# Issuing one buffer's regrouping transfers a step earlier in a spectral-mixing and SoLU kernel

## The chip, the core and the metric

The kernel runs on one core of a Trainium2 chip. A core has five engines with instruction streams of their own: TensorE (PE) multiplies matrices into PSUM, VectorE (DVE) and ScalarE (ACT) do elementwise work, GpSimd (POOL) does elementwise work on SBUF, and SyncE (SP) issues DMA transfers. ACT and POOL can issue transfers too. Each engine works through its instructions in the order in which the program gives them, and waits on semaphores for the other engines and for transfers.

The metric is the time in microseconds of one execution, the median of several.

## The reference

Two blocks follow each other. The first filters along the sequence in the frequency domain, the second is a two-layer network whose activation is `h * softmax(h)` with a layer norm.

```python
# first block: x (8, 3136, 256), filters (1569, 256)
X = np.fft.rfft(x, axis=1)
y = np.fft.irfft(X * (filt_r + 1j * filt_i)[None], n=3136, axis=1)
# second block: x = y as (25088, 256), w_in (256, 1024), w_out (1024, 256)
h = x @ w_in
sm = softmax(h)                      # over the 1024
solu = h * sm
ln = (solu - mean(solu)) / np.sqrt(var(solu) + 1e-6) * g_ln
out = ln @ w_out
```

All of it is float32.

## The kernel before

**Stages.** The Fourier transform is split into matrix products with tables over 49 and 64 points. The sequence of batch element 0 is transformed first. Then one main loop runs, and in it the transforms of elements 1 to 7 are woven between the steps of the network for the tokens that are ready. The table `PLAN` says in which step each piece of a transform stands.

**The network.** The 25,088 tokens are 196 tiles of 128. Two tiles are a *pair* (98 pairs), and two pairs are a *group* (49 groups). For a pair, each of the two layers is computed with seven block products in place of eight (Strassen's scheme in Winograd's form), so sums of blocks are formed by POOL: `pair_sums` for the first layer, `project_sums` for the second.

**Steps.** The main loop calls `step(k)`, with `j, odd = divmod(k, 2)`: two steps, an even and an odd one, for a pair j. One step takes about 7 us. The order of instructions on every engine is the order in which `step` writes them (`tc.manual_schedule()`); no scheduler moves them. A pair goes through these places:

- The first-layer products (line 723) of pair j stand in steps 2j and 2j+1. ACT and DVE bring the results from PSUM to SBUF (`keep`, line 733, and `finish`, lines 744 and 747).
- `exponential` (line 755), `normalize` (line 771), `square` (line 779) and `turn` (line 787) follow for each tile, some steps later. `turn` transposes 32 x 32 blocks on DVE and writes the tile's part of the group's buffer `turn`. The last `turn` of a group with pairs 2g and 2g+1 stands in step 4g+6.
- `regroup(p, i)` (line 799) finishes the transposition with four transfers from `turn` to `solu_t`, from SBUF to SBUF, 128 KB each. There are two destination buffers for a pair, i = 0 and i = 1 (tags `solu_t0`, `solu_t1`), each double-buffered, so that pair p writes where pair p-2 has been. SP issues all of them. Both calls for pair p stand in the even step 2(p+3).
- `deviations` (lines 806 to 810) computes the reciprocal deviations of a group and writes them to DRAM (`rows`) in step 4g+6. `regroup_deviations` (line 816) reads them back with four small transfers, `rs_t`, in the odd step 4g+7. For the last group POOL issues these, otherwise SP.
- `project_sums` (line 702) forms the sums on POOL in step 2(p+4). The first sum reads the second buffer of `solu_t`, and the next the first buffer.
- The second-layer products (line 844) 1, 2, 6 and 7 of pair p stand in the odd step 2(p+4)+1, and products 5, 3 and 4 in the even step after it. Product 1 and 2 read the first buffer of `solu_t`, 4 the second. ACT (`keep_out`, line 856) and DVE (`finish_out`, line 860) scale the results with `rs_t`; the first use of a group's `rs_t` is ACT's instruction after product 1 of the group's first pair. Product 6 adds to the PSUM bank that this ACT instruction reads, so it comes after it.
- `store_out` (line 868) writes the pair's output with two transfers at the end of an even step.

**Other transfers.** SP also issues loads of `x` for the later elements (line 245, four at a time, placed after the stores). ACT issues the loads of `t` (512 KB, line 291) and of the table `de` (line 683), POOL the rest. Transfers of SP and ACT use eight completion semaphores in turn; a transfer that is to use one waits first until the transfer before it on the same semaphore has landed.

**Around the change.** In an odd step the part of `step` that the change touches stands after products 3 and 4 and ahead of `regroup_deviations`; in an even step, after the second-layer product 4 and the loads of `t` and `de`.

Of the kernel before, what the change touches and what calls it, by code (L numbers as in the profile page):

```python
# [94 lines left out]
def kernel(  # L95
# [88 lines left out]
    class Spectrum:  # L184
# [114 lines left out]
        def product(self, i, out, lhsT, rhs):  # L299
            for v in range(self.units[i][1]):  # L300
                nc.tensor.matmul(out=out[:, v, :], lhsT=lhsT(v), rhs=rhs[:, v, :],  # L301
                                 start=True, stop=True)
# [401 lines left out]
    def pair_sums(j):  # L704

        s14 = upool.tile([P, 2, P], FP32, name=f"s14_{j}", tag="s14")
        s23 = wk.tile([P, 2, P], FP32, name=f"s23_{j}", tag="s23")
        sums[j] = s1, s2, s3, s4 = s14[:, 0, :], s23[:, 0, :], s23[:, 1, :], s14[:, 1, :]
        a11, a12, a21, a22 = (tokens(2 * j + i, c) for i in range(2) for c in range(KD))
        sum_of(s1, a21, a22, ALU.add)  # L710
        sum_of(s2, s1, a11, ALU.subtract)
        sum_of(s3, a11, a21, ALU.subtract)
        sum_of(s4, a12, s2, ALU.subtract)
# [15 lines left out]
    def keep(j, k, i):  # L729

        if k not in hs:
            hs[k] = hpool.tile([P, DFF], FP32, name=f"h_{k}", tag=f"h{k % 2}")
        nc.scalar.copy(out=h_half(k, i), in_=ms[j, 0])  # L733

    def finish(j, k, i, kept, bank):


        if k not in nmaxs:
            nmaxs[k] = small.tile([P, 2], FP32, name=f"nmax_{k}", tag=f"nmax{k % 2}")
            sofar, to = 3.0e38, nmaxs[k][:, 0:1]  # L740
        else:
            sofar, to = nmaxs[k][:, 0:1], nmaxs[k][:, 1:2]
        if kept is None:
            nc.vector.tensor_scalar(out=h_half(k, i), in0=ms[j, bank], scalar1=0.0, scalar2=sofar,
                                    op0=ALU.add, op1=ALU.min, accum_out=to)
        else:
            nc.vector.tensor_tensor_reduce(out=h_half(k, i), in0=ms[j, bank], in1=h_half(*kept),  # L747
                                           scale=1.0, scalar=sofar, op0=ALU.add, op1=ALU.min,
                                           accum_out=to)
# [40 lines left out]
    def regroup(p, i):  # L790


        g, second = divmod(p, 2)
        turned = turns[g].rearrange("p (k q) b i -> p k q (b i)", q=4)
        a = 2 * second + i
        st = upool.tile([P, KF, P], FP32, name=f"solu_t_{p}_{i}", tag=f"solu_t{i}")
        solu_ts[p, i] = st[:, 0:KF // 2, :], st[:, KF // 2:KF, :]
        for q in range(4):
            nc.sync.dma_start(out=st[32 * q:32 * q + 32, :, :],  # L799
                              in_=turned[32 * a:32 * a + 32, :, q, :])  # L800
# [17 lines left out]
    def project_sums(p, step):  # L818

        (a11, a12), (a21, a22) = solu_ts[p, 0], solu_ts[p, 1]  # L820
        if step == 0:
            s1 = upool.tile([P, KF // 2, P], FP32, name=f"u1_{p}", tag="u1")
            sum_of(s1, a21, a22, ALU.add)
            sum_of(a21, a11, a21, ALU.subtract)
            solu_sums[p] = s1, None, a21, None
        else:
            s2 = spool.tile([P, KF // 2, P], FP32, name=f"u2_{p}", tag="u2")
            s4 = spool.tile([P, KF // 2, P], FP32, name=f"u4_{p}", tag="u4")
            s1, _, s3, _ = solu_sums[p]
            sum_of(s2, s1, a11, ALU.subtract)  # L830
            sum_of(s4, a12, s2, ALU.subtract)
            solu_sums[p] = s1, s2, s3, s4
# [21 lines left out]
    def keep_out(p, i, to):  # L854
        rs = out_half(p, i, 0)[1]
        nc.scalar.activation(out=out_half(p, *to)[0], in_=pos[p, 0], func=AFT.Copy, scale=rs)  # L856
# [89 lines left out]
    pairs = blocks // 2  # L946

    def step(k):
        j, odd = divmod(k, 2)
        p = j - (LAG - 1) // 2 if odd else j - (LAG + 1) // 2  # L950
        if not 0 <= p < pairs:
            p = None
        hid, proj = k < blocks, p is not None
        if not odd and 2 <= j - 4 < pairs:
            project_sums(j - 4, 0)
        if k < LAG:
            if not odd:
                product(j, 1)
                keep(j, k, 0)
                product(j, 2)  # L960
                finish(j, k, 0, (k, 0), 1)
            else:
                product(j, 5)
                keep(j, k - 1, 1)
                finish(j, k, 1, (k - 1, 1), 2)
        for job in top[k] + stores[k] + products[k]:
            job()
        if not odd and 0 <= j - 4 < 2:
            project_sums(j - 4, 0)
        if odd and j + 1 < pairs:  # L970
            pair_sums(j + 1)
        if not odd:
            if hid and k > LAG:
                product(j, 1)
                keep(j, k, 0)
            if 2 <= k < blocks:
                exponential(k - 2)
            if proj:
                project(p, 5)
                keep_out(p, 1, (0, 1))  # L980
            if blocks <= k < blocks + 2:
                exponential(k - 2)
            if hid and k > LAG:
                product(j, 2)
            if 3 <= k < blocks + 3:
                turn(k - 3)
            if hid and k > LAG:
                finish(j, k, 0, (k, 0), 1)
            if proj:
                finish_out(p, 1, 1, (0, 1), 1)  # L990
            for job in early[k]:
                job()
            if 3 <= k < blocks + 3:
                square(k - 3)
            if hid:
                product(j, 6)
                keep(j, k + 1, 0)
            if proj:
                project(p, 3)
                keep_out(p, 0, (0, 1))  # L1000
                project(p, 4)
            for job in spectrum_loads[k]:
                job()
            if 0 <= j - 3 < pairs:
                regroup(j - 3, 0)
                regroup(j - 3, 1)
            if j - 3 == pairs - 2:
                deviations(j - 3, nc.gpsimd.dma_start)
            if 0 <= j - 4 < pairs:
                project_sums(j - 4, 1)  # L1010
            if j - 3 == pairs - 2:
                regroup_deviations((j - 3) // 2, nc.gpsimd.dma_start)
            elif 0 <= j - 3 < pairs:
                deviations(j - 3, nc.sync.dma_start)
            if hid:
                product(j, 7)
            if 2 <= k < blocks + 2:
                normalize(k - 2)
            for job in second_parts[k] + middle[k] + first_parts[k]:
                job()  # L1020
            if proj:
                finish_out(p, 1, 0, (1, 0), 1)
                store_out(p)
        else:
            if hid and k >= LAG:
                product(j, 5)
                keep(j, k - 1, 1)
                finish(j, k, 1, (k - 1, 1), 2)
            for job in early[k]:
                job()  # L1030
            if proj:
                project(p, 1)
                keep_out(p, 0, (0, 0))
                project(p, 2)
                finish_out(p, 0, 0, (0, 0), 1)
            if 2 <= k < blocks + 2:
                exponential(k - 2)
            if hid:
                product(j, 3)
                product(j, 4)  # L1040
            if 0 <= j - 3 < pairs:
                if (j - 3) % 2 == 0 and j - 3 < pairs - 2:
                    regroup_deviations((j - 3) // 2, nc.sync.dma_start)
            if proj:
                project(p, 6)
                project(p, 7)
            for job in second_parts[k] + middle[k]:
                job()
            if 3 <= k < blocks + 3:
                turn(k - 3)  # L1050
            if hid:
                finish(j, k - 1, 1, None, 0)
                finish(j, k, 0, (k, 0), 2)
            if 2 <= k < blocks + 2:
                normalize(k - 2)
            if proj:
                keep_out(p, 1, (1, 0))
            if 3 <= k < blocks + 3:
                square(k - 3)
            for job in first_parts[k]:  # L1060
                job()
        for job in late[k] + loads[k]:
            job()
        if k < 2:
            for n in ((0, 1), range(2, 7))[k]:
                prepare_w_out(n)
# [37 lines left out]
```

## Time and profile before

The kernel took 1629.31 us, the median of three runs (1626.2 to 1629.95). The profiled execution took 1631.3 us, of which the span from the first to the last instruction is 1629.5.

| engine | busy us | share of the span |
|---|---|---|
| PE | 1551.8 | 95% |
| DVE | 1306.9 | 80% |
| POOL | 1167.1 | 72% |
| ACT | 903.7 | 55% |

| transfers | issued by | how many | KB each |
|---|---|---|---|
| `solu_t` <- `turn`, line 799 | SP | 784 | 128 |
| `out_dram` <- `ot`, line 868 | SP | 196 | 128 |
| `x` <- input, line 245 | SP | 208 | 98 or 128, 16 of 30 |
| `rs_t` <- `rows`, line 816 | SP | 192 | 0.5 |
| `rs_t` <- `rows`, line 816 | POOL | 4 | 0.5 |
| `rows` <- `rs`, line 810 | SP | 48 | 2 |

Busy time is the time in which an engine works on an instruction; issuing a transfer isn't counted. In the lists of waits each line names the waiting engine and line, what it waited for, and the total in microseconds, how often, and the longest. "SPq" is SP's queue of issues. In a timeline a line gives start, length, engine, line, operation and tile of one or more like instructions, and in brackets the idle time before it with what ended it. For a transfer the length is that of its issue by the engine, not that of the data's way.

### The profile page before, as it was taken

Reading aid. Unit: us, or ns where it says so; the run is one execution under the profiler, and the core shown is the slowest. Engines: PE = TensorE matmul, PEld = TensorE weight load, DVE = VectorE, ACT = ScalarE, POOL = GpSimd, SP = SyncE. Lnnn points to the kernel's source line nnn. Section 1 sums busy time; section 2 is a strip of 40 time slices with the busy share of each in tenths; the row PEclk is TensorE's granted clock in tenths of the full one; section 3 lists DMA queues with packets and bytes.
Section 4 is the critical chain, followed back from the end, with each engine's and each line's share of the span. In section 5 each row is a group of like instructions: output and inputs, shape, how many; then the busy total and the mean of one; then the engine's idle time right before and its main releaser. Section 6 shows DMA issues by size and latency. Waiting matters only on the chain.

```text
span 1629.5 us, 37007 instructions
## 1 busy us (share of the span) xinstructions
PE 1551.8 (95%) x12710; PEld 1048.1 (64%) x12710; DVE 1306.9 (80%) x2630; ACT 903.7 (55%) x1772; POOL 1167.1 (72%) x1333
## 2 busy tenths in 40 slices
PE   4898889999999999999999999999999999999997
PEld 1362456666666677667766676666776777777776
DVE  1686778998899889897989888988888777777772
ACT  2235555566565665566656655566556666566662
POOL 4446786688777877697678866788667776677775
PEclk8899999999999999999999999999999999999999
DMA  9887878776888778866787668766875454444443
GB/s 264 251 277 241 237 213 224 216 217 190 208 232 228 205 184 246 225 189 172 207 238 213 187 168 222 230 182 164 224 210 168 128 130 129 104 108 105 112 107 105
DMA packets 377245, 312.13 MB, mean 192 GB/s; under 512 B 62762, under 2 KB 342835, under 8 KB 377059
## 3 DMA queue, kind: packets, MB, share of 16 engines
q1 hardware_dynamic: 304340, 168.63, 40.1%
q0 software_dynamic: 34624, 101.68, 20.9%
q10 hardware_dynamic: 38096, 39.46, 8.2%
q8 instruction: 103, 1.69, 0.4%
q14 instruction: 82, 0.67, 0.1%
HBM read 124.86 MB, written 81.50 MB: 127 GB/s over the span
## 4 chain that ended last, share of the span: by engine, by line
PE 61%; DMA 8%; POOL 3%; DVE 2%; issue 2%; SPq 2%; ACT 1%; ACTq 0%; POOLq 0%; DVEq 0%
PE o L844 28%; PE m L723 27%; DMA solu_t<-turn 4%; PE py L372 3%; PE pa L269 2%; DMA x<-in_x_dram 1%; PE pb L301 1%; PE pc L301 1%; POOL u L702 1%; SPq L799 1%; DMA t<-d 1%; DMA out_dram<-ot 1%; DMA rs_t<-rows 1%; POOL x L260 1%; DVE turn L787 0%
## 5 line engine op out<-in xcount | busy, mean ns | idle before, releaser
L844 PEld LDWEIGHTS o<-w_out_sb,solu_t 128*128 128x128 f32 x3136 | 382.7, 192 | 51.5 <-issue 43.1
L844 PE MATMUL o<-w_out_sb,solu_t 128*128 128x128 f32 x3136 | 402.4, 276 | 4.9 <-DVE ot L860 2.1
L723 PE MATMUL m<-w_in_sb,s 128*128 128x512 f32 x784 | 396.3, 606 | 7.8 <-ACT h L733 7.5
L844 PEld LDWEIGHTS o<-w_out_sb,u 128*128 128x128 f32 x2352 | 308.6, 192 | 144.4 <-issue 105.9
L723 PE MATMUL m<-w_in_sb,y 128*128 128x512 f32 x588 | 309.6, 610 | 11.7 <-DVE nmax L747 9.2
L844 PE MATMUL o<-w_out_sb,u 128*128 128x128 f32 x2352 | 312.9, 276 | 6.2 <-ACT ot L856 3.6
L733 ACT COPY h<-m 128x512 f32<-128x512 f32 x294 | 173.2, 589 | 241.0 <-PE m L723 194.6
L771 DVE SCALAR_TENSOR_TENSOR h<-e,rsum,h 128x1024 f32<-128x1024 f32 x196 | 301.3, 1537 | 6.9
L702 POOL TENSOR_TENSOR u<-solu_t 128x512 f32<-128x512 f32 x98 | 132.9, 1356 | 236.2 <-DMA solu_t<-turn 139.9
L856 ACT ACTIVATE ot<-o,rs_t 128x128 f32<-128x128 f32 x392 | 143.9, 367 | 262.8 <-PE o L844 244.6
L779 ACT ACTIVATE h<-h,nmu 128x1024 f32<-128x1024 f32 x196 | 225.0, 1148 | 58.2 <-DVE turn L787 47.9
L747 DVE CUSTOM_DVE_ANT_0 h<-m,h 128x512 f32<-128x512 f32 x196 | 133.9, 683 | 145.3 <-ACT h L733 104.5
L787 DVE STREAM_TRANSPOSE turn<-h 128x1024 f32<-128x1024 f32 x196 | 243.1, 1240 | 3.2
L755 ACT ACTIVATE e<-h,nmax 128x1024 f32<-128x1024 f32 x196 | 225.2, 1149 | 9.1 <-DVE h L771 8.7
L702 POOL TENSOR_TENSOR u<-solu_t,u 128x512 f32<-128x512 f32 x98 | 150.7, 1538 | 88.4 <-PE o L844 84.1
L723 PEld LDWEIGHTS m<-w_in_sb,s 128*128 128x128 f32 x784 | 128.2, 191 | 95.1 <-issue 85.4
L723 PEld LDWEIGHTS m<-w_in_sb,y 128*128 128x128 f32 x588 | 96.7, 192 | 111.4 <-issue 52.6
L702 POOL TENSOR_TENSOR u<-u,solu_t 128x512 f32<-128x512 f32 x98 | 159.5, 1627 | 0.9
L860 DVE SCALAR_TENSOR_TENSOR ot<-o,rs_t,ot 128x128 f32<-128x128 f32 x294 | 101.8, 346 | 71.7 <-ACT ot L856 51.3
L702 POOL TENSOR_TENSOR solu_t<-solu_t,solu_t 128x512 f32<-128x512 f32 x98 | 152.7, 1558 | 7.7
L702 POOL TENSOR_TENSOR s<-y 128x128 f32<-128x128 f32 x196 | 95.8, 489 | 0.4
L372 PEld LDWEIGHTS py<-wb_t,t 50*64 50x64 f32 x3584 | 57.6, 134 | 42.9 <-issue 21.7
(116 smaller groups left out, 1970.6 us busy)
## 6 DMA issues: line engine op xcount, KB each, us to landing
solu_t<-turn SPq DMA_DIRECT2D x784, 128.0 KB
out_dram<-ot SPq DMA_DIRECT2D x196, 128.0 KB
t<-d POOLq DMA_DIRECT2D x112, 200.0 KB, 6.1
d<-x POOLq DMA_DIRECT2D x100, 200.0 KB, 5.3
f<-f_dram POOLq DMA_DIRECT2D x39, 512.0 KB, 7.0
d<-g POOLq DMA_DIRECT2D x39, 512.0 KB, 4.7
t<-d ACTq DMA_DIRECT2D x37, 512.0 KB
x<-in_x_dram SPq DMA_DIRECT2D x112, 98.0 KB
```

The lines of the kernel that those rows point to most:

```text
L372: nc.tensor.matmul(out=views[g][64 * h:64 * h + 64, cb, i, :], lhsT=t4[rows, i, c0:c0 + 64], rhs=wb_t[rows, 0:N1], start=True, stop=True)
L702: nc.gpsimd.tensor_tensor(out=out, in0=in0, in1=in1, op=op)
L723: nc.tensor.matmul(out=ms[j, bank], lhsT=lhsT, rhs=w_in_sb[:, w, :], start=m in (1, 2, 7), stop=True, skip_group_check=True)
L733: nc.scalar.copy(out=h_half(k, i), in_=ms[j, 0])
L747: nc.vector.tensor_tensor_reduce(out=h_half(k, i), in0=ms[j, bank], in1=h_half(*kept), scale=1.0, scalar=sofar, op0=ALU.add, op1=ALU.min, ...
L755: nc.scalar.activation(out=e, in_=hs[k], func=AFT.Exp, bias=nmaxs.pop(k)[:, 1:2], scale=-1.0, accum_out=esum)
L771: nc.vector.scalar_tensor_tensor(out=solu, in0=e, scalar=rsum, in1=solu, op0=ALU.mult, op1=ALU.mult, accum_out=nmu)
L779: nc.scalar.activation(out=solu, in_=solu, func=AFT.Square, bias=nmu, scale=-float(DFF), accum_out=variances[g][:, i:i + 1])
L787: nc.vector.transpose(out=turns[g][:, :, i, :], in_=solus[k].rearrange("p (f j) -> p f j", j=32))
L844: nc.tensor.matmul(out=pos[p, bank], lhsT=lhs[:, f, :], rhs=w[:, f, :], start=f == 0 and m in (1, 2, 7), stop=True, skip_group_check=True)
L856: nc.scalar.activation(out=out_half(p, *to)[0], in_=pos[p, 0], func=AFT.Copy, scale=rs)
L860: nc.vector.scalar_tensor_tensor(out=ot, in0=pos[p, bank], scalar=rs, in1=out_half(p, *kept)[0], op0=ALU.mult, op1=ALU.add)
```

## The change

For the second pair of each group (odd p), `regroup(p, 0)` moves from the even step 2(p+3) to the odd step before it, 2(p+2)+1, ahead of `regroup_deviations`. `regroup(p, 1)` stays in the even step. For the first pair of a group both calls stay. What is transferred is the same.

```diff
@@ step, even part
             for job in spectrum_loads[k]:
                 job()
             if 0 <= j - 3 < pairs:
-                regroup(j - 3, 0)
-                regroup(j - 3, 1)
+                for i in range((j - 3) % 2, 2):
+                    regroup(j - 3, i)
             if j - 3 == pairs - 2:
                 deviations(j - 3, nc.gpsimd.dma_start)
@@ step, odd part
             if hid:
                 product(j, 3)
                 product(j, 4)
+            if j % 2 and 0 <= j - 2 < pairs:
+                regroup(j - 2, 0)
             if 0 <= j - 3 < pairs:
                 if (j - 3) % 2 == 0 and j - 3 < pairs - 2:
                     regroup_deviations((j - 3) // 2, nc.sync.dma_start)
```

## The prediction

> **What bounds the kernel now.** I write R0 for the four transfers of line 799 into the first buffer (`solu_t`, i = 0) of a group's second pair, R1 for the four into its second buffer, "rs loads" for the four small loads of line 816, and p for the pair number (0 to 97; second pairs are odd). Page first: which engine is full.
>
> ```profile
> span 1629.5 us, 37007 instructions
> ...
> PE 1551.8 (95%) x12710; PEld 1048.1 (64%) x12710; DVE 1306.9 (80%) x2630; ACT 903.7 (55%) x1772; POOL 1167.1 (72%) x1333
> ```
>
> Then the busy time by stage, columns: stretch, length, PE, PEld, DVE, ACT, POOL (each with its count), granted clock, DMA share, GB/s.
>
> ```profile
> 300.00:500.00 200.00, 194.81 (x1743) 132.29 (x1735) 176.37 (x337) 116.15 (x230) 148.79 (x171) 1.00 0.79 215
> ...
> 900.00:1100.00 200.00, 194.24 (x1674) 133.54 (x1674) 170.26 (x336) 116.54 (x230) 147.90 (x172) 0.98 0.72 197
> ...
> 1200.00:1400.00 200.00, 200.00 (x1760) 143.40 (x1753) 160.41 (x348) 119.26 (x235) 139.17 (x159) 1.00 0.54 144
> ```
>
> PE is the bound. From about 1130 us (the last `x` load is issued at 1107.0) its first gap above 0.25 us is at 1587.7, in the drain; a transfer there is worth nothing unless it is late. From 300 to 1100 us it idles 16.2 us in all (800 less 194.81, 196.87, 197.90 and 194.24), and from 165 to 300 another 14.2. So a gain has about 30 us to draw on. Who waits for the transfers concerned (total us, times, longest):
>
> ```profile
> POOL u L702 <- DMA solu_t<-turn: 139.9, 39, 9.9
> ...
> ACT ot L856 <- DMA rs_t<-rows: 14.3, 7, 5.3
> ...
> PEld m L723 <- DVE nmax L747: 23.3, 28, 3.4
> ```
>
> The waits of the SP queue itself, and its order around two second pairs, p = 43 (with `x` loads) and p = 75 (without):
>
> ```profile
> SPq L799 <- DMA t<-d: 42.2, 13, 7.0
> ...
> SPq L816 <- DMA rows<-rs: 29.3, 16, 3.9
> ```
>
> ```profile
> 858.53 1.32 SPq L868 DMA_DIRECT2D out_dram<-ot  x2
> 859.96 2.54 SPq L245 DMA_DIRECT2D x<-in_x_dram  x4
> 863.72 1.74 SPq L816 DMA_DIRECT2D rs_t<-rows  x4
> 865.80 8.29 SPq L799 DMA_DIRECT2D solu_t<-turn  x8
> ```
>
> ```profile
> 1333.35 2.12 SPq L816 DMA_DIRECT2D rs_t<-rows  x4
> 1335.56 7.68 SPq L799 DMA_DIRECT2D solu_t<-turn  x8
> 1343.34 0.61 SPq L868 DMA_DIRECT2D out_dram<-ot  x1
> ```
>
> The reader is to see that R0 and R1 follow the rs loads without a gap: SP is behind, and R0 waits for its place, not for data.
>
> [...] an `rs_t` issue takes 0.42 us (median), its landing comes 4.3 us after it. [...]
>
> **The change part by part.** Nothing is added or removed; 4 × 49 transfers move. PE, ACT, DVE and POOL keep their instruction order. The source is ready: the group's last transpose (line 787) stands one step earlier. The buffer's last reader is product 2 of pair p−2, earlier in the same odd step (for p = 75 it ends at 1330.6), and the wait on it is the same as before. So on SP the order after the stores and `x` loads turns from rs, R0, R1 into R0, rs, R1. For the last pair (p = 97), whose rs loads are issued by POOL, SP's order is unchanged, so the drain's last chain is too.
>
> *R0 earlier*: by the four rs issues, about 1.8 us, plus the wait for `rows`. Who needs R0? POOL's second sum of the pair, which stands behind its first sum, and that reads R1. In every second pair POOL's first sum starts 0.1 to 0.9 us after R1's landing (1345.6 and 1345.7 for p = 75). Worth nothing by itself.
>
> *R1*: still behind both R0 and rs. In the tail it waits for product 4 of pair p−2 (1340.6 for p = 75, R1 issued at 1340.7), so it doesn't move. In the loading stage it starts 0.1 to 8 us after that product (2.0 for p = 33) and could move up by the part of the `rows` wait that R0 now fills. Where a `t` load of 512 KB stands between, SP waits for it (42.2 us in all) before R0's third transfer or so, with five or six issues of 0.65 us behind it; afterwards only two are behind. R1 then lands about 2 us earlier. But PE's gaps that POOL ends come to 4.1 us after 200 us (four, 0.33 to 2.06). Gain: 0 to 4 us; I take 1.5.
>
> *rs later*: by R0's issue, 4 × 0.65 = 2.6 us, and by a second thing. SP and ACT transfers use eight completion semaphores in turn, and a transfer waits until the one before it on its semaphore has landed. In the built program the rs loads follow R1 of the first pair there in 100 of 192 cases before; after, they follow `x` loads in 71, the stores in 53, R0 itself in 20. So where four `x` loads stand ahead, the last rs load is issued only after the last of them landed. The trace's semaphore updates give each landing (the last update on a transfer's semaphore before the next transfer is issued on it), so this can be done pair by pair: last `x` landing + 4.3 us (median landing of `rs_t` before 1130 us, 120 loads, quartiles 3.7 and 5.3), against ACT's first use (line 856). p = 43: 867.2 + 4.3 = 871.5 against 868.3, 3.2 late. p = 33: 711.4 + 4.3 = 715.7 against 714.1, 1.6 late. p = 21: 2.9 late; p = 13: 2.3. Over the 20 second pairs with `x` loads ahead (p = 3 to 59) the lateness is 0.2 to 3.2, in sum about 27 us. In before the same loads land 0.1 to 3.2 us ahead of use; the longest of the seven that came late is
>
> ```profile
> 1059.88 0.37 ACT L856 ACTIVATE ot<-o,rs_t 128x128 f32<-128x128 f32 x1 [5.35 <-DMA rs_t<-rows]
> ```
>
> *What hides it, and what is late next.* Behind the waiting ACT instruction stand the exponential and later evictions, and DVE's line 860. PE's product 6 needs that ACT read, and starts 2.04 us after its end in most groups. DVE's next eviction of a first-layer bank (line 744) ends 0.1 to 2.2 us before PE needs the bank (median about 1.1), with 0.5 us idle before line 860. So 1.1 to 2.0 us are hidden. Taking off each group's own cover (the smaller of 2.0 and 0.5 plus its DVE slack), PE loses 1.8 (p = 21), 2.1 (p = 43), 0.9 (p = 55), 0.8 (p = 29), 0.6 (p = 31, like 55 without cover, since it is late already), 0.4, 0.3 and 0.2: 7.1 us. Without any cover it would be 27. If landing takes 1 us more[...], most groups pass their cover: about 18 us; 2 us more, about 36.
>
> *Tail, p over 60*: no `x` loads. For p = 75: R0 from 1332.4, rs 1335.0 to 1336.9, landed by about 1341.5, used at 1343.3. The slack of 1.9 to 6.8 us before falls by 2.6; only p = 95 (1.9) and the start (p = 1, 0.1) go below nothing. With the drain and the start uncovered: 0.5 and 1.5 us.
>
> **Sum.** +7.1 +2.0 −1.5 = +7.6 us. Against the profiled execution: span 1629.5 to 1637.1, its own time 1631.3 to 1638.9; it lies 2.0 above the median of 1629.3, so the median becomes **1637 us**.
>
> **The rivals.** (1) *R1 sooner, PE fed better: faster.* For it: POOL's 139.9 us of waiting, and 42.2 us of SP waits on `t`. If POOL 2 us earlier also lets its `x` and first-layer sums go sooner, half of the 16.2 us of PE idle goes: 1621 us. It decides if ACT's wait for rs stays under its cover everywhere; against it: PE waited only 4.1 us for POOL, and SP's queue is no shorter. (2) *All of it hidden: no change.* PE absorbed p = 31 in before (ACT 1.5 us late, no PE gap above 0.25 us within 10 us). If rs lands in 3.7 us instead of 4.3, the loss is about 3 + 2.0, less the gain: 1631. (3) *A heavy loss.* Landing of rs behind R0 2 us longer: +36, 1666; with 1 us, 1648. (4) That the order on SP doesn't change is excluded by the built program.
>
> **How the numbers follow.** Small loss as summed, with up to 1 us of longer landing (1634.5 to 1648): 0.45. Heavy loss: 0.13. No change: 0.22. Faster: 0.20. A difference of 0.3% (4.9 us) is about what a measurement can tell from none. The range 1621 to 1654 leaves out the far half of the heavy losses and gains beyond half of the idle time; the likeliest case's own range is 1634 to 1648.
>
> **What would show it.** Right: rs loads behind R0 in the SP timeline; ACT line 856's wait on `rs_t` from 14.3 to 30 us or more, nearly all before 1130 us; PE idle from 300 to 1100 us above 16.2; the tail's PE packed as before; SP's wait on `rows` at line 816 mostly gone. Wrong: ACT's `rs_t` wait about the same, or PE idle smaller with POOL's wait on `solu_t` well under 140 us.

## The result

The changed kernel took 1650.11 us, the median of five runs (1643.86 to 1657.83), against 1629.31 for the kernel before (five runs, 1621.96 to 1632.52): 1.0131 times as long, with a 95% interval of 1.0105 to 1.0156, or 20.8 us more. A loss was forecast and the time lies in the range, but the loss is nearly three times the 7.6 us of the sum. The profiled execution is the slowest of the five: 1657.8 us with a span of 1656.1, 26.6 more than before's span.

First the page's span and busy times, and the busy time by stage (columns as in the prediction).

```profile
span 1656.1 us, 36845 instructions
...
PE 1560.0 (94%) x12710; PEld 1057.3 (64%) x12710; DVE 1287.9 (78%) x2630; ACT 904.3 (55%) x1772; POOL 1159.4 (70%) x1333
```

```profile
300.00:500.00 200.00, 192.74 (x1817) 131.37 (x1810) 170.38 (x336) 115.19 (x228) 145.13 (x173) 0.98 0.78 210
500.00:700.00 200.00, 189.64 (x1732) 130.96 (x1734) 161.84 (x331) 110.84 (x222) 140.80 (x168) 0.97 0.75 209
...
900.00:1100.00 200.00, 194.94 (x1685) 133.11 (x1678) 164.19 (x339) 117.38 (x234) 145.33 (x171) 0.98 0.72 198
...
1200.00:1400.00 200.00, 200.00 (x1798) 143.22 (x1797) 165.42 (x357) 119.12 (x235) 137.98 (x163) 1.00 0.58 158
```

The tail is packed as it was; the loss lies in the stage with `x` loads. The offset between the two executions, taken at the first `keep_out` of a group, grows from +7.1 us at p = 1 to +27.9 at p = 59 and is +25.9 at p = 95.

The 26.6 us can be split without a remainder. PE is busy 1560.0 against 1551.8, so 8.2 us longer for the same 12,710 matmuls, and idle 96.1 against 77.7 (span less busy), so 18.4 us more. Of the idle time 4.0 us fall before 165 us (38.65 against 34.69), where no transfer has moved yet; they belong to this execution and not to the change. 2.0 fall from 165 to 300, 10.9 from 300 to 1100 and 1.5 after it. Without the first 4.0 us, 22.6 are left to explain, close to the 20.8 of the medians.

Now who waits, in the list of waits of the changed kernel.

```profile
POOL u L702 <- DMA solu_t<-turn: 139.0, 49, 8.8
...
ACT ot L856 <- DMA rs_t<-rows: 46.8, 15, 7.6
...
PE o L844 <- ACT ot L856: 28.9, 17, 5.3
...
PEld m L723 <- DVE nmax L747: 7.4, 16, 1.5
```

ACT's wait for `rs_t` went from 14.3 to 46.8 us (another 19.9 are put down to `solu_t`; in this trace 42 of SP's 192 rs loads come next after a `solu_t` transfer on their completion semaphore), and PE's product 6 now waits 28.9 us for that ACT instruction (3.6 before). The wait that shrank is PE's for DVE's `nmax`, from 23.3 to 7.4. The traces of both kernels show what a shared semaphore does: SP and ACT go through eight, and in each trace 1,614 issues come next after another transfer on one, and none begins before that transfer's last update there (0.016 us after it at the least).

The groups of PE's instructions from 300 to 1100 us show both at once: matmuls that read POOL's sums `u` in the second layer (product 6 among them), and the first-layer matmuls that read `y`. Columns: line, operation and tiles, count, busy us and mean ns of one, and after the second bar the idle time just before them with what ended it. Before:

```profile
L844 PE MATMUL o<-w_out_sb,u 128*128 128x128 f32 x1224 | 163.3, 277 | 0.2
L723 PE MATMUL m<-w_in_sb,y 128*128 128x512 f32 x306 | 162.5, 613 | 9.5 <-DVE nmax L747 8.4 <-DVE h L744 1.1
```

After:

```profile
L844 PE MATMUL o<-w_out_sb,u 128*128 128x128 f32 x1184 | 160.9, 280 | 22.9 <-ACT ot L856 22.9
L723 PE MATMUL m<-w_in_sb,y 128*128 128x512 f32 x294 | 155.0, 609 | 1.5 <-DVE nmax L747 0.8 <-DVE h L744 0.6
```

So the change does two things of opposite sign: 22.7 us of new waiting for the rs loads, and some 12.6 us of old waiting that is gone (8.0 here, the rest before other matmuls of lines 723 and 269, whose gaps of 1.2 and 3.4 us went to nothing).

SP's own waits, and its order at the pairs shown before, p = 43 and p = 75:

```profile
SPq L799 <- DMA t<-d: 21.1, 10, 4.7
...
SPq L816 <- DMA solu_t<-turn: 14.8, 12, 3.1
SPq L816 <- DMA x<-in_x_dram: 11.9, 14, 2.7
```

```profile
881.17 1.32 SPq L868 DMA_DIRECT2D out_dram<-ot  x2
882.60 2.21 SPq L245 DMA_DIRECT2D x<-in_x_dram  x4
884.90 3.15 SPq L799 DMA_DIRECT2D solu_t<-turn  x4
888.44 3.60 SPq L816 DMA_DIRECT2D rs_t<-rows  x4
892.14 2.58 SPq L799 DMA_DIRECT2D solu_t<-turn  x4
```

```profile
1357.74 4.12 SPq L799 DMA_DIRECT2D solu_t<-turn  x4
1361.96 2.30 SPq L816 DMA_DIRECT2D rs_t<-rows  x4
1366.56 2.58 SPq L799 DMA_DIRECT2D solu_t<-turn  x4
```

R0, rs, R1, as forecast. The wait of the rs loads for `rows` (29.3 us before) is gone, and in its place they wait for earlier `solu_t` and `x` transfers: the four issues took 1.74 us at p = 43 before and take 3.60 now.

**Where the stalls are.** One group shows the whole chain, p = 29. First SP, then ACT, then PE, then PE's busy time and the granted clock (the third number from the right) in short stretches.

```profile
653.53 3.77 SPq L245 DMA_DIRECT2D x<-in_x_dram  x4
657.40 3.84 SPq L799 DMA_DIRECT2D solu_t<-turn  x4
661.57 3.92 SPq L816 DMA_DIRECT2D rs_t<-rows  x4
665.58 3.50 SPq L799 DMA_DIRECT2D solu_t<-turn  x4
```

```profile
663.56 0.37 ACTq L291 DMA_DIRECT2D t<-d  x1
664.23 1.22 ACTq L683 DMA_DIRECT2D de<-de_tbl  x1
...
673.10 0.37 ACT L856 ACTIVATE ot<-o,rs_t 128x128 f32<-128x128 f32 x1 [7.02 <-DMA rs_t<-rows]
```

```profile
667.59 1.02 PE L723 MATMUL m<-w_in_sb,y 128*128 128x512 f32 x2
673.61 2.04 PE L844 MATMUL o<-w_out_sb,u 128*128 128x128 f32 x8 [4.99 <-ACT ot L856]
```

```profile
664.00:668.00 4.00, 4.00 (x22) 2.74 (x21) 2.52 (x5) 0.58 (x1) 3.12 (x5) 1.00 0.97 291
668.00:672.00 4.00, 0.61 (x2) 0.00 (x0) 0.00 (x0) 0.00 (x0) 1.94 (x5) 0.88 1.09 262
672.00:674.00 2.00, 0.39 (x2) 0.42 (x3) 0.50 (x2) 0.91 (x2) 0.00 (x0) 0.50 0.75 215
674.00:676.00 2.00, 2.00 (x11) 2.00 (x11) 1.97 (x4) 0.90 (x3) 0.34 (x1) 0.50 0.47 156
676.00:678.00 2.00, 2.00 (x15) 1.60 (x17) 2.00 (x4) 1.10 (x2) 1.92 (x2) 0.53 0.55 173
```

The last rs load is issued at 664.6, after ACT has issued the group's 512 KB of `t` and during its issue of the 256 KB of `de`. By the semaphore updates it lands at 673.0, and `de` at 673.5. ACT waits 7.02 us, 2.03 of it are covered, PE stands still for 4.99. After the gap PE runs for about 4 us at half its clock. Before the change all four rs loads of this group were issued by 644.1, and `t` and `de` followed at 646.9 and 647.4:

```profile
638.79 5.31 SPq L816 DMA_DIRECT2D rs_t<-rows  x4
```

### The profile page after: what moved, and what is told of

It reads as the page before. It is cut to its first block, busy times and chain, and to the rows that moved or that the text cites. A ratio compares the mean times of both kernels' runs of the same rounds, so it can differ in the third digit from the quotient of the medians.

```text
span 1656.1 us, 36845 instructions
## 1 busy us (share of the span) xinstructions
PE 1560.0 (94%) x12710; PEld 1057.3 (64%) x12710; DVE 1287.9 (78%) x2630; ACT 904.3 (55%) x1772; POOL 1159.4 (70%) x1333
## 4 chain that ended last, share of the span: by engine, by line
PE 57%; DMA 13%; SPq 3%; DVE 2%; POOL 1%; issue 1%; ACT 0%; POOLq 0%; ACTq 0%; DVEq 0%
PE o L844 26%; PE m L723 25%; DMA solu_t<-turn 6%; DMA x<-in_x_dram 2%; PE py L372 2%; DMA out_dram<-ot 2%; DMA rs_t<-rows 2%; PE pa L269 2%; PE pc L301 1%; SPq L799 1%; PE pb L301 1%; DMA t<-d 1%; POOL u L702 1%; SPq L816 1%; DVE h L771 0%
## 5 line engine op out<-in xcount | busy, mean ns | idle before, releaser
L844 PE MATMUL o<-w_out_sb,u 128*128 128x128 f32 x2352 | 317.2, 279 | 35.8 <-ACT ot L856 28.9
L702 POOL TENSOR_TENSOR u<-solu_t,u 128x512 f32<-128x512 f32 x98 | 147.1, 1501 | 118.2 <-PE o L844 114.0
```

The costliest lines, as they stand in the source:

```text
L702: nc.gpsimd.tensor_tensor(out=out, in0=in0, in1=in1, op=op)
L844: nc.tensor.matmul(out=pos[p, bank], lhsT=lhs[:, f, :], rhs=w[:, f, :], start=f == 0 and m in (1, 2, 7), stop=True, skip_group_check=True)
```

## The experiments

The theory after the result: the rs loads are late, PE pays what exceeds the cover of about 2 us, and the late issue comes from SP's order and from the completion semaphores. Rivals: R0's 512 KB, or R0's early start itself, costs the time; the loss lies in every group and not only where `x` loads stand. All ratios are to the kernel before on the same chip. Where a place of an issue is given "against product 1", it is the mean over the 29 second pairs p = 3 to 59, in one trace, and product 1 is that of the group's first pair.

**The rs loads ahead of R0 again, R0 still in the odd step.**

```diff
-            if j % 2 and 0 <= j - 2 < pairs:
-                regroup(j - 2, 0)
             if 0 <= j - 3 < pairs:
                 if (j - 3) % 2 == 0 and j - 3 < pairs - 2:
                     regroup_deviations((j - 3) // 2, nc.sync.dma_start)
+            if j % 2 and 0 <= j - 2 < pairs:
+                regroup(j - 2, 0)
```

> The change with one line moved: R0 (the four transfers of the second pair's first buffer) still stands in the odd step, but behind the four rs loads of line 816 in place of ahead of them. Theory L (the loss is rs loads that land late because they stand behind R0): the whole loss goes, 1624 to 1634 us, and ACT's waits on rs_t fall back from 46.8 to 12-22 us. Rival Q (the loss comes from R0 leaving the even step as such: the semaphores that transfers share, and the ACT-issued t and de loads that now stand behind R0): the loss stays, 1643 to 1657 us, and ACT's waits on rs_t may fall without the time following.

Measured: 1633.35 us (12 runs), ratio 1.0005 [0.9979, 1.0031]. What costs is that R0 stands ahead of the rs loads; that it belongs to the odd step costs nothing by itself. PE waits 3.7 us before `u` matmuls from 300 to 1100 us, not 22.9. The run does not test R0's early data: SP's order is again rs, R0, R1, and R0 begins 5.3 us ahead of the end of product 1, against 4.9 before and 9.8 in the changed kernel.

**The rs loads issued by POOL, in the changed kernel and in the one before.**

```diff
-                    regroup_deviations((j - 3) // 2, nc.sync.dma_start)
+                    regroup_deviations((j - 3) // 2, nc.gpsimd.dma_start)
```

> The change, with the rs loads of all groups issued by POOL in place of SP, at the same place of the step, so that nothing of theirs stands behind R0. They cost POOL four issues of 0.55 us a group (some 105 us in all) and a wait for rows. Compared with e3, the kernel before with the same edit. Theory L: the two differ by less than 6 us. Rival Q: e2 is 12 to 25 us slower than e3. Both kernels may themselves be some us slower than the kernel before, through POOL.

> The kernel before with the rs loads issued by POOL in place of SP: the control to e2. Theory L and rival Q alike: 1622 to 1640 us, since SP is relieved of 4 issues a group and POOL, busy 72%, takes them; ACT's waits on rs_t 10 to 30 us.

Measured: 1635.58 us, 1.0034 [1.0015, 1.0052], with the change, and 1634.28, 1.0023 [1.0004, 1.0041], without it (20 runs each). With the rs loads out of SP's queue the change costs 1.3 us, not 20.8, and ACT waits 7.4 and 5.6 us for `rs_t`. But SP's order is then the same with and without the change, and R0 begins equally early, 9.6 and 9.5 us ahead of the end of product 1, nearly as early as in the changed kernel (9.8). So it is each ratio to the kernel before that bears on R0's early data: 0.34 and 0.23% more, with the cost of POOL's issues in it (0.55 us each for the last group of the kernel before), so they alone aren't the cause.

**Two of R0's four transfers ahead of the rs loads, two behind; then three and one.** (`regroup` gets a list of quarters.)

```diff
-                regroup(j - 2, 0)
+                regroup(j - 2, 0, range(2))
...
+            if j % 2 and 0 <= j - 2 < pairs:
+                regroup(j - 2, 0, range(2, 4))
```

> The change with R0 cut in two: two of its four transfers ahead of the rs loads, two behind, all in the odd step. Theory L: rs loads are delayed by two issues (1.3 us) in place of four, and PE loses what passes its cover of 1 to 2 us: more than nothing, less than half of the loss, 1632 to 1641 us, ACT's waits on rs_t 22 to 38 us. Rival Q: as with all four ahead, 1643 to 1657.

> The change with three of R0's four transfers ahead of the rs loads and the fourth behind them, in the odd step. With two ahead the loss was gone, with four it was there. Theory L (PE loses what the lateness of rs passes its cover of 1 to 2 us, so the loss grows faster than the number ahead): 1632 to 1645 us, PE's waits for ACT line 856 between the 4.9 us of two ahead and the 28.9 of four. Rival B (the two ahead gain by themselves, and one step more costs nothing until the rs loads follow R0 on its own semaphores, which three ahead mostly avoid): 1620 to 1630.

Measured: two ahead 1624.26 us (7 runs), 0.9972 [0.9942, 1.0002]; three ahead 1634.89 (20 runs), 1.0034 [1.0016, 1.0051]. The first missed its expectation, which had more than nothing and less than half of the loss: two issues ahead of the rs loads cost nothing that shows, though seven runs don't separate this kernel from the one before. The dose is not a straight line: with none, two, three and four transfers ahead it goes 1.0005, 0.9972, 1.0034, 1.0131.

**Two in the odd step ahead of the rs loads, the other two left in the even step.**

```diff
-                for i in range((j - 3) % 2, 2):
-                    regroup(j - 3, i)
+                for i in range(2):
+                    regroup(j - 3, i, range(2 if i == 0 and (j - 3) % 2 else 0, 4))
...
-                regroup(j - 2, 0)
+                regroup(j - 2, 0, range(2))
```

> Two of R0's transfers in the odd step ahead of the rs loads, the other two left in the even step. Theory L: as with two ahead and two behind, rs is 1.3 us later: 1620 to 1634 us. If that kernel's 1624 came from the two behind rs standing in the odd step, this one is slower than it by 3 us or more; if from the two ahead, the same within 3.

Measured: 1624.58 us (20 runs, 1618.25 to 1632.96), 0.9964 [0.9948, 0.9981]. It beats both kernels, by 0.36% the one before. The same two groups of PE's instructions from 300 to 1100 us (the lines of this kernel's code stand four lower):

```profile
L848 PE MATMUL o<-w_out_sb,u 128*128 128x128 f32 x1248 | 165.3, 275 | 3.1 <-ACT ot L860 2.4 <-POOL s L702 0.6
L723 PE MATMUL m<-w_in_sb,y 128*128 128x512 f32 x312 | 164.7, 610 | 0.9 <-DVE h L744 0.6 <-DVE nmax L747 0.3
```

The old gap of 9.5 us before line 723 is gone as in the changed kernel, and the new one is 3.1 us. This profiled execution, of 1619.84 us, is among the fastest of the 20.

**Four small transfers in R0's place.** In the kernel before, four transfers of 512 bytes a group from a constant to DRAM, which nobody reads, are added ahead of the rs loads, or behind them. The output stays the same.

```diff
+    def dummies(g, dma):
+        for b in range(4):
+            to = rs_dram.tile([32, 4], FP32, name=f"dummy_{g}_{b}", tag=f"dummy{b}")
+            dma(out=to, in_=neg_half[32 * b:32 * b + 32, :])
...
+            if (j - 3) % 2 == 0 and 0 <= j - 3 < pairs - 2:
+                dummies((j - 3) // 2, nc.sync.dma_start)
```

The expectation's theory D puts the lateness down to R0's 512 KB themselves.

> The kernel before, with R0 in its old place, and four small transfers of 512 B each added that nobody reads (from a constant tile to DRAM), issued by SP just ahead of the rs loads. They shift the semaphores of the rs loads as the change does (the transfer before them on their semaphore is an x load in 75 cases of 192, a store in 50; with the change 71 and 53), and take SP's time[...]. To be held against e8. Theory S (the lateness comes from the shared semaphores and the issue): e7 is slower than e8 by 8 us or more, ACT's waits on rs_t 30 us or more. Theory D[...]: the two within 5 us, ACT's waits on rs_t below 25 us in both.

> The control to e7: the same four small transfers a group, behind the rs loads. Both theories: ACT's waits on rs_t as in the kernel before, 10 to 22 us, and 1625 to 1638 us, since R0 and R1 stand 1.7 us later in SP's queue, which the trace of before hides in the tail.

Measured: ahead 1700.76 us, 1.0430 [1.0399, 1.0461]; behind 1685.38, 1.0322 [1.0284, 1.0361] (4 runs each). The place is worth 15.4 us, with only 2 KB a group ahead of the rs loads where the changed kernel has R0's 512 KB. The waits with the transfers ahead, and then behind (lines of this code stand five lower):

```profile
ACT ot L861 <- DMA rs_t<-rows: 45.5, 17, 8.2
ACT ot L861 <- DMA solu_t<-turn: 42.4, 10, 10.6
PE o L849 <- ACT ot L861: 40.7, 16, 7.7
```

```profile
POOL u L702 <- DMA solu_t<-turn: 246.7, 47, 12.0
...
PE m L723 <- DVE nmax L747: 31.4, 13, 6.9
...
ACT ot L861 <- DMA rs_t<-rows: 10.5, 5, 3.0
```

Ahead, they make the waits of the changed kernel (45.5 us for `rs_t`, and PE's 40.7). Behind, those waits are gone. That both are far slower than before was a miss and is taken up below.

**The tail alone**: the change for p over 60, then for p over 64.

```diff
-                for i in range((j - 3) % 2, 2):
+                for i in range((j - 3) % 2 if j - 3 > 60 else 0, 2):
...
-            if j % 2 and 0 <= j - 2 < pairs:
+            if j % 2 and 60 < j - 2 < pairs:
```

> The change made for pairs over 60 alone, where no x load stands ahead of the rs loads. Theory L (the loss is rs loads that wait for x loads and R0 in the stage with x loads): the tail has slack, so no loss, 0.998 to 1.002 of before (1626 to 1633 us), ACT's wait on rs_t as in before, about 14 us. Rival (R0 ahead of rs costs in every group): 18 of 48 groups are changed, so three eighths of the loss, about +8 us, 1637.

> As the run with the tail alone, but for pairs over 64 (16 of 48 groups), so that pair 61, whose third rs load waited 6.1 us for a load of t on its completion semaphore there, is as before. If that one place made its loss: 0.999 to 1.002 of before (1628 to 1633 us), no wait of an rs load on t. Rival (R0 ahead of the rs loads costs in every group of the tail): 16/18 of the loss of that run, 1.004, about 1636.

Measured: over 60, 1638.45 us (20 runs), 1.0048 [1.0026, 1.0070], a miss of the theory; over 64, 1628.96 (21 runs), 0.9999 [0.9982, 1.0017]. The two differ in two groups, p = 61 and 63, and at 63 PE has no gap above 0.15 us in the trace of the first. So the loss lies at p = 61. The wait of SP's queue in the first run, and its timeline there, with ACT's:

```profile
SPq L816 <- DMA t<-d: 6.1, 1, 6.1
```

```profile
1131.38 4.21 SPq L799 DMA_DIRECT2D solu_t<-turn  x4
1135.63 8.35 SPq L816 DMA_DIRECT2D rs_t<-rows  x4
```

```profile
1139.47 0.38 ACTq L291 DMA_DIRECT2D t<-d  x1
...
1149.79 0.37 ACT L856 ACTIVATE ot<-o,rs_t 128x128 f32<-128x128 f32 x1 [7.29 <-DMA rs_t<-rows]
```

The rotation of the eight completion semaphores gave the third rs load the one of ACT's next load of `t`. SP stood at that rs load until ACT had issued `t`, 2.4 us later, and `t` had landed at 1143.2. ACT then waited 7.29 us and PE 4.92. It is PE's one gap above 0.25 us from 1110 to 1580 us, and 4.5 us at half clock follow it, so it costs about 7.2 us; the medians of the two kernels differ by 8.4 us and the two profiled spans by 5.3. In the other groups of the tail the change costs nothing that was measured.

**The write of `rows` issued by POOL**, in the kernel before and in the best one, to take one issue a group from SP.

```diff
-                deviations(j - 3, nc.sync.dma_start)
+                deviations(j - 3, nc.gpsimd.dma_start)
```

> The kernel before, but the write of rows (line 810) is issued by POOL in place of SP: one SP issue a group less, no other transfer moved. Theory N (SP's queue is nearly a second bottleneck): SP gets ahead, R1 lands sooner, POOL's wait on solu_t falls below 139 us, PE idle from 300 to 1100 us below 16.2; 0.993 to 0.999 of before, 1618 to 1628 us. Rival (SP's order only matters for rs): within 0.2% of before, 1626 to 1633; or slower, since the issue takes POOL's time (about 1 us a group).

> e9 (two of R0 in the odd step ahead of rs, two in the even step) with the write of rows issued by POOL. Theory N: gains add, 0.990 to 0.996 of before, 1613 to 1623 us. Rival: e9 already has SP on time (first pair's transfers 4 us late in all), so no further gain, 0.996 to 0.998, 1622 to 1626.

Measured: 1638.02 us, 1.0043 [1.0023, 1.0062], and 1634.68, 1.0026 [1.0006, 1.0046] (20 runs each). Both are slower, so this is a miss. SP's wait of the rs loads for `rows` rose from 29.3 to 69.6 us in the first and from 3.6 to 24.6 in the second: `rows` came later. (POOL's own issue of it takes 0.65 us in the kernel before, for the last group.) The idea that each issue taken from SP is a gain gets no support; but this edit changes two things, and doesn't refute it either.

**All kernels side by side.** From the traces, for the 29 second pairs p = 3 to 59: "late" is the landing of the last rs load less the end of product 1 of the group's first pair, and the sum is of what exceeds 2 us. "Behind t, de": groups in which ACT issued a load of `t` or `de` ahead of the last rs load that was still under way when the rs loads began. "Clock" is the sum over slices of 10 us of 10 x (1 - granted clock).

| kernel | profiled execution, us | late beyond 2 us, sum | groups behind t, de | PE idle, 300 to 1100 | clock, 300 to 1100 | ratio |
|---|---|---|---|---|---|---|
| before | 1631.3 | 3.2 | 2 | 16.2 | 3.4 | 1 |
| rs loads first | 1628.5 | 5.0 | 2 | 11.2 | 3.4 | 1.0005 |
| two of R0 ahead, two in the even step | 1619.8 | 3.9 | 2 | 6.2 | 0.0 | 0.9964 |
| two of R0 ahead, two behind | 1620.8 | 3.5 | 1 | 10.1 | 1.7 | 0.9972 |
| three ahead | 1644.6 | 19.1 | 8 | 18.6 | 5.1 | 1.0034 |
| four ahead (the change) | 1657.8 | 26.4 | 8 | 27.0 | 15.3 | 1.0131 |
| small transfers ahead | 1701.6 | 43.3 | 9 | 54.6 | 18.7 | 1.0430 |
| small transfers behind | 1689.5 | 2.2 | 5 | 43.4 | 15.4 | 1.0322 |

The ratio is that of all runs, the columns before it are one execution each, and not always a typical one: with three ahead, with four ahead and with the small transfers behind it is the slowest of its kernel's, with two ahead and two behind the fastest. PE idle from 300 to 1100 us is 16.8 and 16.3 in the two runs of the tail alone, which are like before in this stage.

In the changed kernel the eight groups "behind t, de" hold 24.6 of the 26.4 us; in the kernel with three ahead, all 19.1. That would explain why two ahead cost nothing and four much: the loss comes in a few steps of 3 to 5 us, where the rs loads slip behind the 768 KB that ACT issues. It isn't the whole way: in the four groups that cost most the last rs load lands 8.4 (p = 29), 8.1 (19), 6.0 (53) and 4.9 us (17) after its issue, where 4.3 was typical before, and at 17 and 53 the issue itself had to wait for the landing of R0's second transfer, the one before it on its semaphore. No run moved `t` and `de` alone, so that link rests on the traces. Part of it lies in the rotation, by the order of use of each semaphore: before, 12 loads of `de` from 165 to 1150 us came next after an rs load on their semaphore and so could not be issued ahead of it, and 11 of them were issued within 0.6 us of its landing (p = 29: landing 647.2, issue 647.4). In each of the kernels with two of R0 ahead there are 6 such loads, with three and with four ahead none.

## Why the prediction was half right

**The order on SP, and the signs.** Right. All five signs came: rs behind R0, ACT's wait for `rs_t` at 46.8 (30 or more), PE idle at 27.0 (over 16.2), the tail at 200.00 of 200, the wait for `rows` at 0.7 us.

**rs later.** Right in kind. Over the 29 groups the last rs load lands 3.10 us later against product 1 (from -1.67 to +1.43 in the mean). Of this the first issue makes 2.03 (the step said 2.6), the issue of the four 1.22 (2.72 to 3.94, the wait on `x` and `solu_t` semaphores), and the landing after the last issue -0.17. So the longer landing that rival 3 feared from R0's data is not there in the mean; the 1 and 2 us that it took for it were my estimate, which no trace had shown. Two experiments show that it is the place of the rs loads on SP that costs: rs first (1.0005) and the small transfers (15.4 us by place alone). In the groups behind `t` and `de` the last rs load lands close to these two, within 1.2 us of the later in six of the eight (0.5 us at p = 29), and 1.8 and 2.0 us after it in the others. That isn't a proof that they hold it back.

**The sum of lateness is the term that failed.** The step had eight groups with 7.1 us beyond the cover, from "last x landing + 4.3". Measured are 25.4 us, PE's 28.9 us of waiting for ACT's instruction less the 3.48 of the start. Of the five groups that the step names, p = 21 and 31 lost nothing (1.8 and 0.6 were forecast), p = 55 lost 0.28 (0.9), p = 29 lost 4.99 (0.8) and p = 43 lost 2.03 (2.1). The last came about as said: its last rs load landed 4.15 us after its issue, near the 4.3 of the step. The four that cost most are p = 17, 19, 29 and 53, with gaps of 4.79, 5.31, 4.99 and 4.51. The typical landing of 4.3 us came from loads that `t` and `de` followed; I didn't ask what ACT would issue in the 3 us by which the rs loads move. In the kernel before, the one group behind both loads was also the latest, p = 55 with the wait of 5.35 us that the prediction shows: the sign was there.

**The cover.** Right: of the seven groups 1.4 to 2.2 us late with p = 3, 9, 13, 21, 35, 47 and 57, PE lost 0.22 us at most in any.

**The clock was missing.** A stall was counted at its own length. The gaps before about 472, 513, 674 and 1051 us are each followed by some microseconds at a granted clock near 0.5: by the table's measure 15.3 us against 3.4 from 300 to 1100 us. Counted only while PE works, with half of each us at a granted clock of 0.5 as lost, it is 11.4 us against 3.4 there, and 21.6 against 14.2 in the whole span (8.7 against 7.6 of it before 165 us). So most of PE's 8.2 us of longer busy time is the clock, and it stands beside 18.4 us more of idle time.

**R1 sooner, 1.5 us, was too small.** The landing did move 2.1 us, as said (11.35 to 9.25 after product 4 of pair p-2, in the mean). The step priced it by PE's gaps that POOL ended, 4.1 us. But the chain seems to go on: POOL's next first-layer sums, then the matmuls, then DVE's `nmax`, with the gap of 9.5 us ended by DVE at its end. That gap goes with R1's landing after product 1 in most kernels: 8.5 us and a gap of 9.5 before, 7.6 and 2.0 with rs first, 6.4 and 1.5 in the changed kernel, 10.2 and 29.5 with the small transfers behind; with these ahead, 9.6 and 7.8, it doesn't. No run moved R1 alone. SP also gains: the first pair's transfers of the next group started 38.2 us late in all against the last `turn` before, and 5.7 after. The best kernel shows the worth, PE idle 6.2 against 16.2 us. Rival 1, at 1621 us, had this gain, and said that it decides if ACT stays under its cover: with two transfers moved it does (1624.58).

**Tail and start.** Right that the tail loses nothing, and the run for p over 64 confirms it. The start (p = 1) was priced at 1.5 us; PE's gap before product 6 there went from 0.38 to 3.48 us, the one before product 1 from 1.80 to 0.83. But the slack of 1.9 to 6.8 us that the step leans on is no guarantee: one rotation of the semaphores made ACT wait 7.29 us at p = 61 in the run for p over 60.

**The number in the range is partly luck.** The losses were priced too low by some 26 us (25.4 less 7.1, and 8.2 for the clock), the gain by 11.1 (12.6 less 1.5), and the two errors take each other off in part. With the gain as priced, the kernel would have been near 1661 us, an estimate from these numbers, outside the range to 1654.

## What to carry to other kernels

When an issue is moved on a DMA queue, ask of each small load behind it not only how much later it is issued, but which large transfer of another queue it then falls behind (the last rs load of p = 29 landed 8.4 us after its issue, where 4.3 was typical), and which transfer comes before it on its completion semaphore (at p = 61, in the run for p over 60, a load of `t`, for which SP stood 6.1 us). Price a stall of a saturated PE with the clock that follows it: after the 4.99 us at p = 29, PE ran some 4 us at 0.50 to 0.53. And try half the move: here two of the four transfers gave the gain alone (0.9964 and 0.9972), three 1.0034 and four 1.0131.

## What the runs showed that was not expected

**Half clock after short gaps.** In the changed kernel the half clock stands at the four long gaps of PE (for the 4.99 us to 673.6: 0.50 to 0.53 for 6 us, to 678). But shorter ones brought it too: after the gap of 2.03 us that ends at 895.7 the clock was 0.50 from 897 to 899, and in the kernel before after 2.57 us (to 1059.1) 0.53 from 1062 to 1064. A gap of 2.06 us, to 481.7 in before, left it at 1.00. Of the eight gaps of 2.0 to 2.9 us from 250 to 1580 us in the kernels before, changed and with three ahead, five brought it; one of 2.01 us did, and one of 2.83 us did not. So among these gaps the length alone doesn't decide.

From 165 to 1600 us in these two kernels, before and changed, the half clock comes in stretches of 3.4 or 6.8 us. The four gaps of 4.5 to 5.3 us of the changed kernel have 6.8 us each, and PE works in 4.3 to 6.0 us of them. The gap of 2.03 us has 3.4 us, which begin at 896.3, when PE is at work again.

**Small transfers on SP are not small.** 192 transfers of 512 bytes behind the rs loads cost 56 us (1685.38 less 1629.45), 0.29 us each, though their data are 96 KB in all. The waits of SP's queue at these transfers (line 815) show a part of it:

```profile
SPq L815 <- DMA t<-d: 47.7, 11, 7.8
...
SPq L815 <- DMA out_dram<-ot: 34.1, 23, 4.2
```

They take their turn among the eight semaphores and wait there for loads of `t` (47.7 us) and stores (34.1), and R0 and R1 stand behind: POOL's wait for `solu_t` went from 139.9 to 246.7 us. How much of the 56 us is this and how much their plain issue was not separated.
